# v of five tile pairs by seven half-width products, with staging buffers in the order k, v, q

## The chip, the cores and the metric

The kernel runs on one core of a Trainium2 chip. The metric is the device time in microseconds of one execution; smaller is better.

## The reference

The part that matters is how q, k and v are made and used. `x` has 2048 rows of 512; the weight `wqkv` has 512 columns each for q, k and v; there are 32 heads of 16, and each row attends to 8 rows of its past, two apart.

```python
xn = layernorm(x)                                  # 2048 x 512
q, k, v = split(xn @ wqkv)                         # 512 x 1536, 32 heads of 16
logits = einsum("bhsd,bhswd->bhsw", q, k[s - 2*w]) * 16**-0.5     # w = 0..7, masked at the start
o = einsum("bhsw,bhswd->bhsd", softmax(logits), v[s - 2*w])
s = o @ wo                                         # 512 x 512
h = relu(xn @ w1 + b1) ** 2                        # 1792 wide
out = x + s * silu(h @ w2 + b2)
```

## The kernel before

**Tiles and stages.** The rows are 16 tiles of 128. The first stage normalizes tiles, transposes them, and multiplies them by `wqkv`; from tile 2 on it takes them in pairs (2, 4, ... 14). q, k and v go to DRAM through staging buffers `stg` (a ring of four; 128 partitions, both tiles of a pair) and come back in another layout as the attention's units of 256 rows. The second stage is the feed-forward part in four chunks of 512 rows, with the attention on VectorE (DVE) beside it and the output products `pw` at the end of each chunk.

**Precision.** Every operand of a matmul is split in a high part, rounded by ScalarE (ACT), and a low part, the rest, subtracted by DVE or GpSimd (POOL). A product of high and low parts takes three matmuls, `PASSES`: high by high, high by low, low by high. So the low part of x is wanted from the third matmul on, the low part of a weight from the second.

**The pair of seven.** Pairs 4 to 14 (`SEVEN`, L43) compute q and k together as a product of 2 by 2 blocks: rows of tile a and of tile b, halves of the contraction (`part_x(t, 0)` and `part_x(t, 1)`), columns of q and of k. By Winograd's scheme this takes seven block products instead of eight, each of six matmuls of 512 columns (`product`, L536). The scheme needs sums of x blocks (`sums`, L504, on DVE from PSUM; their parts by `high_sums` on ACT and `low_sums` on DVE) and four sums of weights, T1 to T4, made by DVE and POOL before pair 2 and split during it (`split_sum`, low halves on POOL). The text counts the products of a pair in the order of the code:

1. x of a, first half, by Q0, into `sums_ps`; ACT copies it to `first`, which must be done before product 3 adds to `sums_ps`.
2. the sum S0 by T1, into `five`.
3. S1 by T2, on top of `sums_ps`; evacuated as u, into a buffer of its own (`u2`).
4. x of a, second half, by Q1, on top of `first`: q of tile a.
5. S2 by T3, on top of `sums_ps`; POOL adds it to k of tile b.
6. S3 by K1, on top of `five`; DVE adds u: k of tile a. k is stored.
7. x of b by T4, on top of `sums_ps`: q of tile b. q is stored.

v of the two tiles is computed beside that by `qkv(t, 2)` (L551): 12 matmuls of 512 columns a tile, into a bank of its own, evacuated by ACT.

**What sets the order.** Every engine runs its instructions in the order in which the code issues them (`Ordered`, L75; `queue` does it for SyncE's transfers), and each waits for its operands. Between products stands `beside(a, step)` (L735), which first issues what a table has for that place (`at`, L700), then `pump(LATE)` (L371): as much of the attention as a planner's two clocks, one for TensorE and one for DVE, leave room for. The table makes the statistics, the norms, the transposes (`trans`, `highx`, `lowx`) and the sums for later pairs. At place (2, 2) it has `trans(4)`, `trans(5)`, `stats(6)`, `stats(7)`, `norm(6)` and the split of T3; at (2, 3) `highx`, `norm(7)` and the split of T4; at (2, 4) `lowx(4)`, the sums of x for pair 4 and `spread(8)`; at (2, 5) their rest and `spread(9)`. `spread(t)` (L418) is the statistics of a tile on ACT: a Copy and a Square with an accumulator each, whose 512-wide results are not used, and three small operations on POOL.

**The banks.** PSUM has eight banks: four for accumulators (`psA`), two for `psH`, two for transposes. The raw weights of v, `raws[2]`, lie in the buffer that the attention's v tiles take later. Buffers 10 and `K0` are taken by the pieces 0 and 1 of the feed-forward weights (`next_w`, L394; `HOME`, L41).

Of the kernel before, what the change touches and what calls it, by code (L numbers as in the profile page):

```python
# [14 lines left out]
P = 128  # L15
S = 2048
D = 512
# [25 lines left out]
SEVEN = range(4, 16, 2)  # L43

# [7 lines left out]
MATMUL, TRANSPOSE, DVE_FIXED, SHARED, SLACK, LATE, ROOM0, ROOM = 227, 150, 150, 200, 500, 3000, 500, 3500  # L52
# [5 lines left out]
def body(ctx: ExitStack, tc: tile.TileContext, x, wqkv, wo, w1, b1, w2, b2, out):  # L58
# [5 lines left out]
    def price(engine, name, a, k):  # L64
        if engine == "PE":
            return MATMUL if name == "matmul" else TRANSPOSE
# [178 lines left out]
    def attention():  # L245
# [121 lines left out]

    stream = attention()
# [167 lines left out]
    def product(ps, lhs, w, start=True):  # L536

        k = 0
        for i in range(2):
            for p, q in PASSES:  # L540
                PE.matmul(ps, lhs(p, i), wq[w][:, q, i, :], start=start and k == 0, stop=k == 5,
# [3 lines left out]
    def heads(ps):  # L545
        return ps.rearrange("p (g c) -> p g c", g=GR)
# [4 lines left out]
    def qkv(t, s, between=None, late=False):  # L551
# [10 lines left out]
        evacuate(t, s, ps)  # L562

    def evacuate(t, s, ps):
        if t % 2 == 0:
# [122 lines left out]

    qkv(1, 2)
# [38 lines left out]
    for i, w in enumerate((T2, T3, T4)):  # L728
        at(2, 1 + i, split_sum, w, G)
    for i in range(2):  # L730
        at(4, i, load_w, i)

    ahead = {(10, 2): 1, (12, 4): 1, (14, 0): 1, (14, 2): 1, (14, 4): 1}

    def beside(a, step):  # L735
# [3 lines left out]
        for n in range(ahead.get((a, step), 0)):  # L739
            next_w()  # L740
        pump(LATE)
# [15 lines left out]
    def pair_of_seven(a):  # L757

        b, last = a + 1, a + 2 == NT
        new_stg(a, 1)  # L760
        new_stg(a, 0)
        q, k = stgs[0], stgs[1]
        sums_ps, first, five = (psA(f"pm{a}_{n}") for n in range(3))
        home = dict(pool=px, tag="x", bufs=4) if last else dict(pool=hpool, tag="hf")
        u2 = home.pop("pool").tile([P, GR, CH], F32, name=f"u2_{a}", **home)
# [10 lines left out]
        A.activation(q[:, :, 0], heads(first), AF.Copy)  # L776
        beside(a, 2)
# [234 lines left out]
```

## Time and profile before

| | us |
|---|---|
| median of 3 runs (487.14 to 488.4) | 487.44 |
| profiled execution | 488.73 |
| its span (first to last instruction) | 486.8 |
| TensorE busy | 478.8 (98%) |
| VectorE busy | 417.6 (86%) |
| ScalarE busy | 235.1 (48%) |
| GpSimd busy | 204.1 (42%) |
| pairs 4 to 12 | 41.8 to 119.6 |

Times in the views are microseconds from the span's start. PE is TensorE's matmuls, PEld its weight loads, DVE VectorE, ACT ScalarE, POOL GpSimd, SP SyncE. A group's row gives output and input by the program's names, partitions by elements, the count, busy time and the mean in ns, then the engine's idle time just before it and what ended it. A row of a timeline gives start and length; several like instructions in a row are merged (x4). Matmuls are pipelined: one takes some 0.39 us from start to end, but the next starts earlier, so the pace is read from long rows. All instructions of the main engines carry the line of a helper (L87), so they are told apart by names: `pm` is a pair's products, `pq` a plain `qkv`, `pb` and `ph` the feed-forward part, `pr` and `pv` the attention's products on DVE, `S` and `Sf` the sums of x, `wqraw` raw weights and their sums, `wq` weight parts, `xt` x parts.

### The profile page before, as it was taken

What the parts mean: (1) busy time and instruction counts of PE and PEld (TensorE: products, weight loads), DVE (VectorE), ACT (ScalarE), POOL (GpSimd) and SP (SyncE); (2) the same over time, 40 slices, a digit from 0 to 9 for tenths busy, and PEclk for the clock granted to TensorE, in tenths of its full rate; (3) what the DMA queues carried; (4) which work ended last, traced back from release to release, by engine and by line L of the source; (5) the groups of instructions that cost most, each with busy time, mean ns of one, the idle gap of its engine ahead of it and who ended that gap; (6) DMA issues with size and microseconds to landing.
All of it is one profiled execution on the core that took longest, in us unless ns stands there. A gap on an engine that the chain in (4) does not pass through costs nothing.

```text
span 486.8 us, 5931 instructions
## 1 busy us (share of the span) xinstructions
PE 478.8 (98%) x2118; PEld 393.8 (81%) x2118; DVE 417.6 (86%) x348; ACT 235.1 (48%) x421; POOL 204.1 (42%) x166
## 2 busy tenths in 40 slices
PE   8999999999999999999999999999999999999996
PEld 5888788886888888888888888888888888888885
DVE  5967968986869699999999999999989999959533
ACT  5548697645575576453422444343233543423240
POOL 1347232132756699235534332653524145353210
PEclk9999999999999999999999999999999999999999
DMA  7999999898757992943708184425723852330142
GB/s 278 248 247 275 308 303 260 200 277 276 218 160 197 254 226 91 254 130 68 193 18 200 53 227 139 102 86 125 182 72 71 270 125 86 82 102 27 49 138 76
DMA packets 71002, 81.47 MB, mean 167 GB/s; under 512 B 6204, under 2 KB 55612, under 8 KB 70972
## 3 DMA queue, kind: packets, MB, share of 16 engines
q1 hardware_dynamic: 65788, 54.87, 40.8%
q10 hardware_dynamic: 5184, 26.22, 22.1%
q8 instruction: 17, 0.28, 0.3%
q14 instruction: 13, 0.11, 0.1%
HBM read 50.60 MB, written 27.32 MB: 160 GB/s over the span
## 4 chain that ended last, share of the span: by engine, by line
PE 87%; DMA 5%; DVE 4%; ACT 2%; issue 1%; SPq 0%; POOL 0%; DVEq 0%; ACTq 0%; POOLq 0%
PE pb L87 31%; PE ph L87 31%; PE pq L87 10%; PE pw L87 9%; PE pm L87 5%; DMA sk<-stg 2%; DMA sx<-xt 1%; DVE L L87 1%; DMA xb<-xn 1%; DMA x<-in_A_x 1%; DVE pxT L87 1%; SPq L100 0%; ACT stg L87 0%; DVE pr L87 0%; ACT mean L87 0%
## 5 line engine op out<-in xcount | busy, mean ns | idle before, releaser
L87 PE MATMUL pb<-w,h 128*128 128x512 f32 x672 | 160.1, 389 | 0.0
L87 PEld LDWEIGHTS pb<-w,h 128*128 128x128 f32 x672 | 126.1, 188 | 26.2
L87 POOL TENSOR_TENSOR h<-hf,h 128x512 fp32r<-128x512 f32 x46 | 72.5, 1576 | 152.0 <-ACT hf L87 152.0
L87 PE MATMUL ph<-xU,w 128*128 128x512 f32 x504 | 120.2, 389 | 0.0
L87 ACT ACTIVATE ph<-ph,b1t 128x512 f32<-128x512 f32 x56 | 37.0, 661 | 161.4 <-PE ph L87 152.7
L87 PEld LDWEIGHTS ph<-xU,w 128*128 128x128 f32 x504 | 94.6, 188 | 19.6
L87 DVE TENSOR_TENSOR pr<-k,q 128x2048 f32<-128x2048 f32 x32 | 78.9, 2466 | 4.4 <-DMA q<-sq 3.9
L87 DVE TENSOR_TENSOR pv<-v,L 128x2048 f32<-128x2048 f32 x32 | 75.4, 2355 | 6.3 <-POOL L L87 5.5
L87 DVE TENSOR_REDUCE v<-pv 128x256 f32<-128x2048 f32 x32 | 73.0, 2281 | 0.8
L87 DVE TENSOR_REDUCE L<-pr 128x128 f32<-128x2048 f32 x32 | 72.9, 2279 | 0.7
L87 PE MATMUL pw<-wot,oT 128*128 128x512 f32 (+1 forms) x204 | 45.9, 376 | 0.0
L87 PEld LDWEIGHTS pw<-wot,oT 128*128 128x128 f32 x204 | 36.8, 188 | 7.1
L87 PE MATMUL ph<-xT,w 128*128 128x512 f32 x168 | 40.0, 389 | 0.0
L87 PE MATMUL pq<-wq,xt 128*128 128x512 f32 x144 | 36.0, 392 | 1.7 <-ACT stg L87 1.7
L87 PEld LDWEIGHTS ph<-xT,w 128*128 128x128 f32 x168 | 31.5, 188 | 6.5
L87 PE MATMUL pm<-wq,S 128*128 128x512 f32 x144 | 35.9, 391 | 0.1
L87 POOL TENSOR_TENSOR w<-w1r,w 128x512 fp32r<-128x512 f32 x14 | 22.4, 1598 | 29.1 <-ACT w L87 29.1
L87 ACT ACTIVATE h<-ph 128x512 fp32r<-128x512 f32 x56 | 33.7, 602 | 1.7
L87 PEld LDWEIGHTS pq<-wq,xt 128*128 128x128 f32 x144 | 26.8, 188 | 8.3 <-ACT stg L87 2.8
L87 PEld LDWEIGHTS pm<-wq,S 128*128 128x128 f32 x144 | 26.8, 188 | 6.4 <-ACT u L87 0.7
L87 PE MATMUL pq<-wq,xT 128*128 128x512 f32 x132 | 30.9, 393 | 0.0
L87 PEld LDWEIGHTS pq<-wq,xT 128*128 128x128 f32 x132 | 24.5, 188 | 5.8 <-ACT xT L87 0.7
(82 smaller groups left out, 486.8 us busy)
## 6 DMA issues: line engine op xcount, KB each, us to landing
k<-sk ACTq DMA_DIRECT2D x8, 960.0 KB, 7.4
v<-sv ACTq DMA_DIRECT2D x8, 960.0 KB, 7.5
sx<-xt SPq DMA_DIRECT2D x12, 512.0 KB, 5.7
xU<-sx ACTq DMA_DIRECT2D x12, 512.0 KB, 7.2
x<-in_A_x SPq DMA_DIRECT2D x16, 256.0 KB, 6.3
sk<-stg SPq DMA_DIRECT2D x8, 512.0 KB, 4.3
sq<-stg SPq DMA_DIRECT2D x8, 512.0 KB, 7.3
sv<-stg SPq DMA_DIRECT2D x8, 512.0 KB, 5.0
```

Of the source, the lines that this page charges most:

```text
L87: return tc.keep_in_program_order(f(*a, **k))
```

## The change

v of tiles 4 to 13 (pairs 4 to 12, `VSEVEN`) is computed as q and k are, with blocks of 256 columns: the left and right half of v take the places of q and k. So a pair has seven more products of six matmuls, each 256 wide (`cols`), in place of 24 matmuls of 512. The v product n stands right behind product n (`first_v` is the first, with its copy to `v_first`; `sixth` is product 5 with its evacuation and POOL's add, `seventh` product 6 with DVE's add and the store of k). The four sums of v's weights are made on DVE at place (2, 2), in place in `raws[2]` (`sum_v`), and split at (2, 4), (2, 5), (4, 0) and (4, 1) (`split_v`: high parts ACT, low parts POOL) into buffers 10 and K0. The splits of the feed-forward pieces 0 and 1 move from (10, 2) and (12, 4) to (12, 3) and (12, 5), and the first load of an attention v tile waits until place (4, 1) is issued. All three staging buffers of a pair are taken at its start, in the order k, v, q. u goes to k's own buffer. The unused results of `spread` go to a buffer in SBUF, which frees the two `psH` banks for v.

```diff
-MATMUL, TRANSPOSE, DVE_FIXED, ...
+MATMUL, VMATMUL, TRANSPOSE, DVE_FIXED, ... = 227, 120, 150, 150, ...
...
-        yield from load(0, "kqv")
+        yield from load(0, "kq")
...
+                    if u == 0 and s == 1:
+                        while not v_ready:
+                            yield None
+                        yield from load(0, "v")
...
-        A.activation(psH(f"mean{t}"), xins[t], AF.Copy, scale=-1.0 / D, accum_out=means[t])
-        A.activation(psH(f"var{t}"), xins[t], AF.Square, bias=means[t], accum_out=rs[t])
+        waste = hpool.tile([P, 512], F32, name=f"waste{t}", tag="hf")
+        A.activation(waste, xins[t], AF.Copy, scale=-1.0 / D, accum_out=means[t])
+        A.activation(waste, xins[t], AF.Square, bias=means[t], accum_out=rs[t])
...
+    def sum_v(n):
+        dst, a, b = (((0, vl), (0, vr), (0, vl)), ((2, vr), (2, vr), (0, vl)), ((0, vr), (2, vr), (0, vr)),
+                     ((2, vl), (2, vl), (2, vr)))[n]
+        dst, a, b = (raws[2][:, kt:kt + 2, cols] for kt, cols in (dst, a, b))
+        V.tensor_sub(dst, a, b)
+        v_sums[n] = dst
+
+    def split_v(n):
+        i = n // 2
+        if i not in v_parts:
+            v_parts[i] = buffer(f"vsum{i}", (10, K0)[i])
+        split(*(v_parts[i][:, q, :, (vl, vr)[n % 2]] for q in range(2)), v_sums[n], G)
...
+    for a, step, f, n in ((2, 2, sum_v, 0), (2, 2, sum_v, 2), (2, 2, sum_v, 1), (2, 2, sum_v, 3),
+                          (2, 4, split_v, 0), (2, 5, split_v, 1), (4, 0, split_v, 2), (4, 1, split_v, 3)):
+        at(a, step, f, n)
...
-    ahead = {(10, 2): 1, (12, 4): 1, (14, 0): 1, (14, 2): 1, (14, 4): 1}
+    ahead = {(12, 3): 1, (12, 5): 1, (14, 0): 1, (14, 2): 1, (14, 4): 1}
...
+        for s in (1, 2, 0):
+            new_stg(a, s)
+        q, k, v = (stgs[s] for s in range(3))
...
         product(sums_ps, part_x(a, 0), Q0)
         A.activation(first, sums_ps, AF.Copy)
+        if seven:
+            first_v()
         product(five, part_s(a, 0), T1)
         A.activation(k[:, :, 1], heads(five), AF.Copy)
+        if seven:
+            product(v_five[:, vl], part_s(a, 0), v_parts[0], cols=vl)
+            A.activation(v[:, 4:, 1], heads(v_five[:, vl]), AF.Copy)
         beside(a, 0)
-        qkv(a, 2)
-        beside(a, 1)
+        if not seven:
+            qkv(a, 2, new=False)
+            beside(a, 1)
         product(sums_ps, part_s(a, 1), T2, False)
-        A.activation(u2, heads(sums_ps), AF.Copy)
+        A.activation(k[:, :, 0], heads(sums_ps), AF.Copy)
+        if seven:
+            product(v_sums_ps[:, vl], part_s(a, 1), v_parts[0], False, vr)
+            A.activation(v[:, 4:, 0], heads(v_sums_ps[:, vl]), AF.Copy)
+            beside(a, 1)
...
+        if seven:
+            sixth()
+            product(v_sums_ps[:, vl], part_s(a, 2), v_parts[1], False, vl)
+            A.activation(v[:, :4, 1], heads(v_sums_ps[:, vl]), AF.Copy)
+            G.tensor_add(v[:, 4:, 1], v[:, 4:, 1], v[:, :4, 1])
+            beside(a, 3)
+            seventh()
+            product(v_five[:, vl], part_s(a, 3), V1, False, vr)
+            not_before(clock["PE"])
+            V.tensor_add(v[:, 4:, 0], v[:, 4:, 0], heads(v_five[:, vl]))
...
+        if seven:
+            product(v_sums_ps[:, vl], part_x(b, 1), v_parts[1], False, vr)
+            A.activation(v[:, :4, 1], heads(v_sums_ps[:, vl]), AF.Copy)
+            store_qkv(b, 2)
         store_qkv(b, 0)
```

More of the change, by code (lines that the diff above doesn't have):

```diff
@@ L43 @@
 SEVEN = range(4, 16, 2)
+VSEVEN = range(4, 14, 2)
 WARM = 18
@@ L50 @@
 STATS = 8
[L52 removed]
+MATMUL, VMATMUL, TRANSPOSE, DVE_FIXED, SHARED, SLACK, LATE, ROOM0, ROOM = 227, 120, 150, 150, 200, 500, 3000, 500, 3500
 BEHIND, FREE, LAND, LOAD = 5000, 2000, 4500, 10500
@@ L534, in part_s, with product @@
         return lambda p, i: Sp[a, j // 2][:, p, j % 2, i]
-    def product(ps, lhs, w, start=True):
+    def product(ps, lhs, w, start=True, cols=slice(0, 512)):
         k = 0
+        w = wq[w] if isinstance(w, int) else w
         for i in range(2):
             for p, q in PASSES:
-                PE.matmul(ps, lhs(p, i), wq[w][:, q, i, :], start=start and k == 0, stop=k == 5,
+                PE.matmul(ps, lhs(p, i), w[:, q, i, cols], start=start and k == 0, stop=k == 5,
                           skip_group_check=True)
@@ L545, in heads, with qkv @@
     def heads(ps):
-        return ps.rearrange("p (g c) -> p g c", g=GR)
+        return ps.rearrange("p (g c) -> p g c", c=CH)
     def new_stg(t, s):
         stgs[s] = pstg.tile([P, GR, 2, CH], F32, name=f"stg{t}_{s}", tag="stg", bufs=4)
-    def qkv(t, s, between=None, late=False):
+    def qkv(t, s, between=None, late=False, new=True):
         ps = psA(f"pq{t}_{s}")
@@ L561, in qkv, with evacuate @@
                 between()
-        evacuate(t, s, ps)
-    def evacuate(t, s, ps):
-        if t % 2 == 0:
+        evacuate(t, s, ps, new)
+    def evacuate(t, s, ps, new=True):
+        if t % 2 == 0 and new:
             new_stg(t, s)
@@ L740, in beside @@
             next_w()
+        if (a, step) == (4, 1):
+            v_ready.append(True)
         pump(LATE)
```

43 lines of the change are left out of this document (29 added, 14 removed).

## The prediction

> **What bounds the kernel now.** I read the page first, then the table of stretches for the five pairs that the change rewrites (one row each, start and end of the pair's matmuls), then the timelines of single engines around places where TensorE waits.
>
> ```profile
> PE 478.8 (98%) x2118; PEld 393.8 (81%) x2118; DVE 417.6 (86%) x348; ACT 235.1 (48%) x421; POOL 204.1 (42%) x166
> ...
> PE 87%; DMA 5%; DVE 4%; ACT 2%; issue 1%; SPq 0%; POOL 0%; DVEq 0%; ACTq 0%; POOLq 0%
> ...
> L87 PE MATMUL pq<-wq,xt 128*128 128x512 f32 x144 | 36.0, 392 | 1.7 <-ACT stg L87 1.7
> ```
> ```profile
> 41.78:56.88 15.10, 15.10 (x67) 12.26 (x66) 12.99 (x16) 10.58 (x23) 8.09 (x9) 1.00 1.10 309
> 56.88:72.80 15.92, 15.32 (x67) 12.31 (x66) 11.16 (x19) 15.07 (x35) 5.09 (x13) 1.00 1.10 295
> 72.80:87.87 15.07, 15.07 (x67) 12.31 (x66) 12.68 (x15) 11.08 (x25) 4.81 (x8) 1.00 0.81 219
> 87.87:102.83 14.96, 14.96 (x67) 12.39 (x66) 12.74 (x20) 9.47 (x18) 4.67 (x3) 1.00 1.10 266
> 102.83:119.56 16.73, 15.58 (x67) 12.23 (x66) 12.54 (x15) 6.89 (x14) 1.29 (x1) 1.00 0.94 270
> ```
>
> TensorE is busy 98% of the span and carries 87% of the chain, so a microsecond taken from its work, or added to its waits, is a microsecond of the result. Columns of the table: stretch, length, busy time and count for PE, PEld, DVE, ACT, POOL, then granted clock, DMA share, GB/s. A pair without a wait takes 14.96 us (pair 10). Pairs 6 and 12 take 15.92 and 16.73: 0.96 and 1.77 us of waiting.
>
> **Streaming.** The price of a full matmul comes from the chain in order of time, that of a half-width one from the last two output products, which are 256 wide already.
>
> ```profile
> 458.36 2.72 PE pb L87 x12
> ```
> ```profile
> L87 PE MATMUL pw<-wot,oT 128*128 128x256 f32 x24 | 3.0, 283 | 0.0
> ```
> ```profile
> 480.10:482.50 2.40, 2.40 (x23) 2.40 (x22) 2.18 (x4) 0.00 (x0) 0.00 (x0) 1.00 0.05 11
> ```
>
> A 512-wide matmul costs 2.72/12 = 0.227 us. Of 24 half-width ones, 23 steps fit into 3.0 - 0.28 us: 0.118; some 20 whole steps in 2.40 us say 0.120, and the weight loads (x22, busy without a gap) set that pace, not the columns. I take 0.120. A pair's v goes from 24 x 0.227 = 5.44 us to 7 x 6 x 0.120 = 5.04: 0.40 less, over five pairs **-2.0 us**. By the Trainium skill (TensorE: Matmul & The Clock Gate, Back-to-back issue gap) a warm matmul of N columns is spaced N/2.4 + 2.5 ns, 109 ns here; by that estimate the five pairs would save 4.3 us, but the rows above show 120, bound by the loads.
>
> **Waits that may go.** Before 112 us the v evacuation held ACT, and TensorE behind it:
>
> ```profile
> 111.57 0.60 ACT L87 ACTIVATE stg<-pq 128x512 f32<-128x512 f32 x1 [5.22 <-DMA sk<-stg]
> ```
>
> v's staging buffer was still being stored. In the new pair v's first write comes after the fourth group of matmuls (1.36 + 0.72 + 1.36 + 0.72 = 4.2 us), and v's sums have banks of their own, so ACT can be several us late without stopping TensorE. Of the 2.73 us in pairs 6 and 12 I take **-2.3** (between 0 and -2.7).
>
> **The entry to pair 4.** Here the change adds work to three queues that are already late. DVE must still make, in this order, norm(6), the four subtractions for v's weight sums, norm(7), lowx(4), and the sums of x that pair 4 multiplies.
>
> ```profile
> 36.94 0.69 DVE L87 BATCH_NORM_STATS2 st<-x 128x6 f32<-128x512 f32 x1 [2.13 <-DMA x<-in_A_x]
> ...
> 37.95 0.54 DVE L87 TENSOR_SCALAR xn<-x,mv,rs 128x512 f32<-128x512 f32 x1
> 38.94 1.51 DVE L87 TENSOR_SCALAR xn<-x,mv,rs 128x512 f32<-128x512 f32 x1 [0.44 <-POOL rs L87]
> 40.38 0.68 DVE L87 TENSOR_TENSOR xt<-pxT,xt 128x512 fp32r<-128x512 f32 x1
> ...
> 45.61 2.29 DVE L87 TENSOR_TENSOR pr<-k,q 128x2048 f32<-128x2048 f32 x1
> ```
> ```profile
> 38.88 5.69 POOL L87 TENSOR_TENSOR wq<-wqraw,wq 128x512 fp32r<-128x512 f32 x4
> 44.65 0.19 POOL L87 TENSOR_SCALAR rs<-rs 128x1 f32<-128x1 f32 x1
> 44.92 0.55 POOL L87 TENSOR_TENSOR rs<-rs,mhalf 128x1 f32<-128x1 f32 x1
> 45.55 0.19 POOL L87 TENSOR_TENSOR shift<-mean,rs 128x1 f32<-128x1 f32 x1
> 46.52 1.43 POOL L87 TENSOR_SCALAR rs<-rs 128x1 f32<-128x1 f32 x1 [0.77 <-ACT var L87]
> ```
> ```profile
> L87 DVE TENSOR_TENSOR wqraw<-wqraw,wqraw 128x512 f32<-128x512 f32 x6 | 3.7, 683 | 0.0
> ```
>
> norm(6) frees DVE at about 38.4. A subtraction of 512 elements costs 3.7/6 = 0.6 us when alone, so four would be 2.5 us. They are not alone: at 38.88 POOL begins the four low halves of T3 and T4 (5.69 us). What such a meeting does is shown at 121 us, DVE's and POOL's timelines:
>
> ```profile
> 121.24 0.68 DVE L87 TENSOR_TENSOR L<-L,sm 128x256 f32<-128x256 f32 x1
> 121.84 3.38 DVE L87 TENSOR_TENSOR pr<-k,q 128x2048 f32<-128x2048 f32 x1
> ```
> ```profile
> 121.60 1.47 POOL L87 TENSOR_TENSOR w<-w2r,w 128x512 fp32r<-128x512 f32 x1
> 123.68 2.70 POOL L87 TENSOR_TENSOR w<-w1r,w 128x512 fp32r<-128x512 f32 x1 [0.60 <-ACT w L87]
> ```
>
> pr takes 2.29 us at 45.61 and 3.38 here, ending 2.15 us after POOL's subtraction ended at 123.07; POOL's next one, issued at 123.68, ends at 126.38, 1.2 us after pr. And POOL got in between two DVE operations that stood back to back. So operations that read two SBUF operands go one at a time and in turn. The Trainium skill (SBUF — State Buffer, Who interferes with whom) says the same, that the shared pair is held for a whole instruction and the other engine blocks fully; the rows agree, and it is a rule that speaks against this placing.
>
> In turn, then: first subtraction to 39.0, POOL to 40.25, DVE to 40.8, POOL to 42.05, DVE to 42.6, POOL to 43.85, DVE to 44.4, POOL to 45.65 (1.25 and 0.55 each), and norm(7), which waited for POOL in the same way (1.51), to 45.95. lowx(4) starts at 45.9 instead of 40.38: **5.5 us later**. The ends: 1.0 if DVE keeps its turn four times and norm(7) then meets no POOL operation (38.4 + 2.5 + 0.5 = 41.4), 6 if POOL always goes first. The rows at 121 us are the nearest; I take 5.5.
>
> What waits for it:
>
> ```profile
> 41.78 1.52 PE L87 MATMUL pm<-wq,xt 128*128 128x512 f32 x6
> ...
> 47.36 1.52 PE L87 MATMUL pm<-wq,S 128*128 128x512 f32 x6
> ```
> ```profile
> 41.87 0.63 ACT L87 ACTIVATE S<-Sf 128x512 fp32r<-128x512 f32 x1 [1.95 <-DVE Sf L87]
> ...
> 43.78 0.19 ACT L87 ACTIVATION_READ_ACCUMULATOR var<-x,mean 128x1 f32 x1
> 43.87 0.58 ACT L87 ACTIVATE stg<-pq 128x512 f32<-128x512 f32 x1
> 44.35 0.62 ACT L87 ACTIVATE S<-Sf 128x512 fp32r<-128x512 f32 x1
> ...
> 46.24 0.19 ACT L87 ACTIVATION_READ_ACCUMULATOR var<-x,mean 128x1 f32 x1
> 46.34 0.58 ACT L87 ACTIVATE pm<-pm 128x512 f32<-128x512 f32 x1
> ```
>
> Pair 4's first product needs the low part of x from its third matmul on (41.78 + 0.45 = 42.23); it comes at 46.6, and TensorE stands 4.3 us. ACT's queue hangs on DVE's sums (idle 1.95 until 41.87), so its whole row above moves by 5.5, and two new high parts of v's sums (0.52 each, as 43.87 to 44.35 and 44.35 to 44.87 go) stand ahead of the copy of the first product: 46.34 + 5.5 + 1.04 = 52.9, done at 53.5. In the old order that copy was wanted at 47.36, now before product 3, and product 3 now stands earlier: without waits at 45.94. POOL: the second group of small operations starts when var(9) is there (46.43 + 5.5 + 0.52 = 52.45), takes 1.1 us (44.65 to 45.74), then the low part of split_v(1) 1.3: 54.9. The third v product needs it, and ends at 55.6. Without waits it ends at 41.78 + 3 x 1.36 + 3 x 0.72 = 48.0. The entry costs **+7.6 us**. With no delay on DVE at all, ACT's two new operations alone make the copy ready at 46.9 + 1.04 = 47.95, where 45.94 is wanted: +2.0. That is the lower end. The upper: a pr in front of POOL's group (46.52 took 1.43 instead of 0.19, because pr ran) adds 1.4: 9.0.
>
> **At nothing.** A pair's evacuations on ACT become six of 256 instead of two of 512, on DVE one add is new, on POOL one. Each result is wanted 2.8 us or more after its product, and ACT has 4 us free in pairs 8 and 10; were the cover gone, each late 0.4 us evacuation would show as such.
>
> ```profile
> L87 ACT ACTIVATE Sf<-pxT 128x256 f32<-128x256 f32 x6 | 2.4, 403 | 0.0
> ```
>
> The statistics' waste goes from PSUM to SBUF at equal length. DVE's extra 4.5 us (4 x 0.6, 5 x 0.42) meets a tail with room: the last low part ends at 470.6, its tile's products start one product after 477.24, which leaves over 6 us. The v load of unit 0 goes behind pair 4's second step; cover is the rest of unit 0's logits on DVE, and its price if needed at once is its landing, 7.5 us. The splits of weight pieces 0 and 1, moved to pair 12, go past no evacuation that product 7 waits for, and the loads of pieces 2 and 3 that they start are wanted after pair 14. u in k's own buffer is the same ACT copy to another place.
>
> ```profile
> 469.91 0.69 DVE L87 TENSOR_TENSOR oT<-pT,oT 128x512 fp32r<-128x512 f32 x1 [1.32 <-ACT oT L87]
> ```
> ```profile
> 477.24 5.75 PE L87 MATMUL pw<-wot,oT 128*128 128x512 f32 x36
> ```
> ```profile
> v<-sv ACTq DMA_DIRECT2D x8, 960.0 KB, 7.5
> ```
>
> **Sum.** -2.0 - 2.3 + 7.6 = +3.3 us. Against the profiled execution (488.73: span 486.8 and 1.9 around it) that is 492.0; that execution lies 1.3 above the median of 487.44, so in terms of the median **490.7**.
>
> **Rivals.** *The turns do not alternate* (0.38). DVE's four subtractions run through while POOL waits: the delay is 0 to 1.0 and the entry costs 2.0 to 3.0 us, or POOL gets in once or twice, 3.0 to 5.5. For it: four DVE operations of one kind, each ready when the last ends. Against: pr at 121.84 was ready too and waited. With 2.0 and the waits gone the time is 487.4 - 4.3 + 2.0 = 485.1, faster; with 4.3 it is no change. The point is an entry of 2.8 us, 485.9: below it the change wins by over 0.3% (about what a measurement of this kernel can tell from no change). I give the faster part 0.21, the middle 0.17. *The entry drops TensorE's clock* (0.10). The last row of stretches shows the clock at 0.51 after 2.4 us without matmuls:
>
> ```profile
> 485.40:486.80 1.40, 0.00 (x0) 0.00 (x0) 0.00 (x0) 0.00 (x0) 0.00 (x0) 0.51 0.00 0
> ```
>
> A stop of 4.3 us is longer. If the clock takes as long to come back as the stop lasted, 4.3 us at half pace lose 2.1, unless they fall into the waits that follow: 492.8. The Trainium skill (TensorE: Matmul & The Clock Gate, The HAM clock gate) gives one idle window of about 3.4 us for the fall and as much work for the rise; by that estimate it would be 1.7 us, and the 0.51 agrees with its idle state. *The DMA waits move* (0.07). v now takes the buffer from which the last pair's k is stored; if that lands 1 us too late in each of four pairs and the old 2.3 stays: 490.7 + 2.3 + 4 = 497.
>
> **How the numbers follow.** Main case 0.45, its own range 489.0 to 492.6; with the two slow rivals slower gets 0.62. Faster 0.21, same 0.17. The range, 485.0 to 493.0, reaches from the lower end of the first rival to the clock's case; the DMA case and what lies outside both ends are left out.
>
> **What would show it.** 256-wide pm and pv matmuls at 0.120; the four wqraw subtractions on DVE spread over 5 to 6 us between POOL's; lowx(4) near 46; TensorE idle in the first product of pair 4 and before its second and third v product; pairs 6 to 12 at 14.6 us. Wrong would be: subtractions 0.6 us apart, or a pair 4 under 17 us.

## The result, and the profile after

The changed kernel is slower by 1.28%: 494.4 us (median of 4 runs, 494.05 to 494.89) against 487.9 on the same chip, a ratio of 1.0128 with the interval 1.0097 to 1.0159. Its profiled execution took 494.3 us, span 492.5; the one before had 488.73 and 486.8. From the first matmul of pair 14 to the last of the kernel both take 363.2 us, and pair 4 starts at 41.8 in both, so the whole difference between the two profiled executions lies in the five pairs that were rewritten.

The table of stretches of the changed kernel, pairs 4, 6, 8, 10 and 12 (stretch, length, busy time and count of PE, PEld, DVE, ACT, POOL, then granted clock, DMA share, GB/s):

```profile
41.80:66.24 24.44, 17.11 (x86) 14.07 (x85) 17.44 (x24) 16.51 (x37) 15.91 (x17) 0.93 0.72 186
66.24:80.94 14.70, 14.70 (x87) 12.90 (x86) 12.77 (x16) 13.13 (x32) 4.73 (x11) 1.00 0.93 255
80.94:95.79 14.85, 14.85 (x86) 12.96 (x85) 14.55 (x20) 12.26 (x29) 5.92 (x10) 1.00 1.05 256
95.79:110.49 14.70, 14.70 (x87) 12.90 (x85) 14.10 (x21) 9.32 (x20) 5.15 (x4) 1.00 1.04 279
110.49:125.19 14.70, 14.70 (x87) 12.90 (x85) 11.76 (x14) 8.53 (x20) 3.78 (x4) 1.00 0.99 286
```

Before they took 15.10, 15.92, 15.07, 14.96 and 16.73, 77.78 in all; now 83.39, or 5.61 more, which is the difference of the two profiled executions (5.57). Four pairs became shorter by 3.7 together, and pair 4 longer by 9.3. The page shows the same as a small loss of TensorE's share and a dent in the fourth and fifth slice:

```profile
PE 479.4 (97%) x2208; PEld 398.6 (81%) x2208; DVE 427.3 (87%) x357; ACT 242.4 (49%) x445; POOL 221.4 (45%) x175
PE   8996799999999999999999999999999999999996
PEclk9998999999999999999999999999999999999999
```

Pair 4 on TensorE's timeline (start, length, operation, what ended the idle time before it):

```profile
41.80 0.61 PE L90 MATMUL pm<-wq,xt 128*128 128x512 f32 x2
46.75 2.08 PE L90 MATMUL pm<-wq,xt 128*128 128x512 f32 x4 [4.33 <-DVE xt L90]
48.62 1.40 PE L90 MATMUL pv<-wq,xt 128*128 128x256 f32 x6
50.65 1.65 PE L90 MATMUL pm<-wq,S 128*128 128x512 f32 x6 [0.63 <-ACT stg L90]
52.14 0.87 PE L90 MATMUL pv<-vsum,S 128*128 128x256 f32 x6
53.64 1.66 PE L90 MATMUL pm<-wq,S 128*128 128x512 f32 x6 [0.62 <-ACT pm L90]
55.13 0.28 PE L90 MATMUL pv<-vsum,S 128*128 128x256 f32 x1
57.15 0.86 PE L90 MATMUL pv<-vsum,S 128*128 128x256 f32 x5 [1.75 <-POOL vsum L90]
57.85 1.54 PE L90 MATMUL pm<-wq,xt 128*128 128x512 f32 x6
```

There are four stops: the first is ended by DVE, the next two by ACT, the last by POOL. After that nothing holds the pair. An undisturbed full product and the half-width one behind it take 2.10 together (14.70/7), so the fourth product would start at 41.80 + 3 x 2.10 = 48.10; it starts at 57.85. The entry costs 9.75 us.

### The profile page after: what moved, and what is told of

Read it like the earlier page. It is cut to its first block, busy times and chain, and to the rows that moved or that the text cites. A ratio compares the mean times of both kernels' runs of the same rounds, so it can differ in the third digit from the quotient of the medians.

```text
span 492.5 us, 6172 instructions
## 1 busy us (share of the span) xinstructions
PE 479.4 (97%) x2208; PEld 398.6 (81%) x2208; DVE 427.3 (87%) x357; ACT 242.4 (49%) x445; POOL 221.4 (45%) x175
## 4 chain that ended last, share of the span: by engine, by line
PE 90%; DMA 4%; DVE 2%; ACT 1%; POOL 1%; issue 0%; SPq 0%; POOLq 0%; ACTq 0%
PE pb L90 31%; PE ph L90 31%; PE pm L90 11%; PE pw L90 9%; PE pv L90 5%; PE pq L90 4%; DMA x<-in_A_x 2%; DMA sq<-stg 2%; DVE wqraw L90 1%; POOL vsum L90 1%; DVE xn L90 0%; ACT waste L90 0%; DVE st L90 0%; PE pxT L90 0%; POOL rs L90 0%
## 5 line engine op out<-in xcount | busy, mean ns | idle before, releaser
L90 POOL TENSOR_TENSOR h<-hf,h 128x512 fp32r<-128x512 f32 x46 | 83.8, 1822 | 138.7 <-ACT hf L90 137.9
L90 PE MATMUL pw<-wot,oT 128*128 128x512 f32 (+1 forms) x204 | 45.9, 376 | 0.0
L90 PE MATMUL pm<-wq,S 128*128 128x512 f32 x144 | 37.1, 394 | 1.2 <-ACT stg L90 0.6
L90 POOL TENSOR_TENSOR w<-w1r,w 128x512 fp32r<-128x512 f32 x14 | 26.0, 1860 | 18.9 <-ACT w L90 16.3
L90 PE MATMUL pm<-wq,xt 128*128 128x512 f32 x108 | 29.1, 404 | 4.3 <-DVE xt L90 4.3
L90 PEld LDWEIGHTS pm<-wq,S 128*128 128x128 f32 x144 | 25.8, 189 | 6.1 <-ACT stg L90 0.8
L90 ACT ACTIVATE hf<-ph 128x512 f32<-128x512 f32 x46 | 27.3, 594 | 1.9 <-POOL h L90 1.9
```

Of the source, the lines that this page charges most:

```text
L90: return tc.keep_in_program_order(f(*a, **k))
```

## Where pair 4 lost its time

DVE's timeline, and POOL's beside it:

```profile
38.94 5.75 DVE L90 TENSOR_TENSOR wqraw<-wqraw 128x512 f32<-128x512 f32 x4
44.61 1.48 DVE L90 TENSOR_SCALAR xn<-x,mv,rs 128x512 f32<-128x512 f32 x1
46.01 0.68 DVE L90 TENSOR_TENSOR xt<-pxT,xt 128x512 fp32r<-128x512 f32 x1
...
53.72 2.26 DVE L90 TENSOR_TENSOR pr<-k,q 128x2048 f32<-128x2048 f32 x1
```
```profile
39.41 6.40 POOL L90 TENSOR_TENSOR wq<-wqraw,wq 128x512 fp32r<-128x512 f32 x4
...
52.67 0.19 POOL L90 TENSOR_SCALAR rs<-rs 128x1 f32<-128x1 f32 x1 [0.64 <-ACT waste L90]
...
53.72 4.63 POOL L90 TENSOR_TENSOR vsum<-wqraw,vsum 128x512 fp32r<-128x512 f32 x2
```

The four subtractions take 5.75 us beside POOL's four low halves, and `lowx(4)` starts at 46.01: the turns, as forecast (45.9). The last row of POOL is new. There the low part of `split_v(1)` starts in the same moment as DVE's `pr` and stands behind it; it ends at about 57.1. The row has two such operations in 4.63 us; in other kernels two take 2.5 us when nothing holds them. TensorE's last stop ends then, at 57.15. ACT's timeline joins the two ends:

```profile
47.51 0.63 ACT L90 ACTIVATE S<-Sf 128x512 fp32r<-128x512 f32 x1 [7.57 <-DVE Sf L90]
...
49.50 0.61 ACT L90 ACTIVATE vsum<-wqraw 128x512 fp32r<-128x512 f32 x1
50.02 0.58 ACT L90 ACTIVATE stg<-pq 128x512 f32<-128x512 f32 x1
...
52.49 0.62 ACT L90 ACTIVATE vsum<-wqraw 128x512 fp32r<-128x512 f32 x1
53.01 0.58 ACT L90 ACTIVATE pm<-pm 128x512 f32<-128x512 f32 x1
```

ACT is idle 7.57 us for the sums of x (1.95 before). Then come a spread, a new high part and only then `stg<-pq`, the evacuation of pair 2's last product; the second product of pair 4 (50.65) takes the bank that this one empties. Another spread and another new high part stand ahead of `pm<-pm`, the copy of the first product, which releases the third (53.64). Where the forecast had one late copy on ACT, there are two. From 47.51 to 53.5 ACT works without a gap, and POOL's small operations wait for ACT and not for TensorE; so the low part comes at 57.1 however early TensorE gets there, and the last stop, not the sum of the four, sets the 9.75.

The clock fell as well. A stretch of the same table, just behind the first stop:

```profile
46.70:49.70 3.00, 2.95 (x10) 2.57 (x10) 2.69 (x6) 2.16 (x6) 0.02 (x1) 0.50 0.72 146
```

Ten matmuls (the rest of the first product and its half-width one) ran at half the granted clock. At full pace they would have ended at about 48.4 (4 x 0.227 + 0.72 from 46.75) instead of 50.0; since the next product waited until 50.65 anyway, nothing of this reached the end.

## The experiments

The pair lengths of all kernels, from their profiled executions, with the sum of the five, the median time, and the ratio to the kernel before on the same chip (the experiments ran on several chips, where the kernel before took 487.85 to 488.15):

| kernel | pair 4 | 6 | 8 | 10 | 12 | sum | median | ratio (interval) |
|---|---|---|---|---|---|---|---|---|
| before | 15.10 | 15.92 | 15.07 | 14.96 | 16.73 | 77.8 | 487.9 | 1 |
| changed | 24.44 | 14.70 | 14.85 | 14.70 | 14.70 | 83.4 | 494.4 | 1.0128 (1.0097 to 1.0159) |
| order alone | 15.31 | 15.67 | 15.78 | 14.96 | 14.96 | 76.7 | 487.98 | 1.0006 (0.9987 to 1.0025) |
| no low halves of T3, T4 | 17.42 | 14.70 | 14.85 | 14.70 | 14.70 | 76.4 | 487.86 | 0.9997 (0.9983 to 1.0012) |
| sums earlier | 20.16 | 14.70 | 14.84 | 14.69 | 14.82 | 79.2 | 490.2 | 1.0057 (1.0031 to 1.0084) |
| no sums | 19.09 | 14.70 | 17.45 | 15.97 | 14.70 | 81.9 | 494.31 | 1.0129 (1.004 to 1.0217) |
| no sums, priced | 20.41 | 14.70 | 14.85 | 14.70 | 14.70 | 79.4 | 491.25 | 1.0072 (1.0046 to 1.0098) |
| `split_v(1)` first | 22.75 | 14.70 | 14.85 | 14.69 | 14.70 | 81.7 | 493.52 | 1.0109 (1.0072 to 1.0145) |
| early sums and splits | 19.25 | 14.70 | 14.85 | 14.70 | 14.70 | 78.2 | 489.47 | 1.0038 (1.002 to 1.0057) |
| from pair 6 | 14.99 | 16.50 | 14.70 | 14.70 | 14.70 | 75.6 | 487.03 | 0.9981 (0.9965 to 0.9998) |
| from 6, end of 4 later | 15.33 | 16.49 | 14.70 | 14.70 | 14.70 | 75.9 | 486.79 | 0.9977 (0.9958 to 0.9996) |
| from 6, one spread less | 14.99 | 14.98 | 15.64 | 14.70 | 14.70 | 75.0 | 486.75 | 0.9969 (0.995 to 0.9987) |
| from 6, two by two | 15.09 | 16.50 | 15.40 | 14.64 | 14.81 | 76.4 | 487.31 | 0.9983 (0.9959 to 1.0006) |

**Order alone: everything but the products.** Staging order, u, waste, the later load of v and the later splits stay; the half-width products, their sums and splits go.

```diff
-VSEVEN = range(4, 14, 2)
+VSEVEN = range(0)
...
-    for a, step, f, n in ((2, 2, sum_v, 0), (2, 2, sum_v, 2), (2, 2, sum_v, 1), (2, 2, sum_v, 3),
-                          (2, 4, split_v, 0), (2, 5, split_v, 1), (4, 0, split_v, 2), (4, 1, split_v, 3)):
-        at(a, step, f, n)
```

> The changed kernel without its half-width products: v by two plain products of 12 full matmuls a tile as before, no sums of v's weights; the staging order k, v, q, u in k's buffer, the waste in SBUF, the later v load and the later feed-forward splits stay. Theory (the waits of pairs 6 and 12 went because v is written later and has its own banks): they are still there, pairs 4 to 12 take together 77 to 78.5 us, the time is 487 to 489. Rival (the staging order alone frees the buffer in time): pairs 6 and 12 come down to 15.0, the time is 485 to 486.

It took 487.98 us, no change to measure, as the theory had it. The pairs divide it from the rival less clearly: their sum is 76.7, below the 77 to 78.5 of the theory, because the wait of pair 12 is not in this profile (14.96), while those of ACT in pair 6 and now pair 8 are (15.67 and 15.78). So the rearrangement without the products neither costs nor brings anything that can be measured in the time.

**No low halves of T3 and T4.** POOL does not make them; products 5 and 7 take the high half in their place.

```diff
+        only_high = isinstance(w, int) and w in (T3, T4)
...
-                PE.matmul(ps, lhs(p, i), w[:, q, i, cols], start=start and k == 0, stop=k == 5,
+                PE.matmul(ps, lhs(p, i), w[:, 0 if only_high else q, i, cols], start=start and k == 0, stop=k == 5,
...
-            split(*sum_weights[w, i], eng)
+            (high(*sum_weights[w, i]) if w in (T3, T4) else split(*sum_weights[w, i], eng))
```

> The changed kernel without POOL's four low halves of T3 and T4; products 5 and 7 use the high half in the low half's place, so q and k are less exact. DVE's four subtractions stay where they are. Theory (turns): the subtractions stand 0.6 us apart, 2.5 us in all, norm(7) is not held either, lowx(4) starts near 42; POOL has no queue, so the low parts of v's sums come earlier too; the time is 487 to 489. Rival (the subtractions are slow by themselves, for instance because they write over what they read): still 5 to 6 us in all, lowx(4) near 46, the time above 492.

The subtractions on DVE's timeline, without POOL beside them:

```profile
37.94 2.87 DVE L90 TENSOR_TENSOR wqraw<-wqraw 128x512 f32<-128x512 f32 x4
41.18 0.68 DVE L90 TENSOR_TENSOR xt<-pxT,xt 128x512 fp32r<-128x512 f32 x1
```

They take 2.87 us instead of 5.75, `norm(7)` behind them is not held either, and `lowx(4)` starts at 41.18 instead of 46.01. Pair 4 falls from 24.44 to 17.42, and the time to that of before. These 7.0 us are not the turns alone, for the run also takes 5.7 to 6.4 us of work out of POOL's queue. POOL's low part of `split_v(1)` comes just ahead of `pr`, and this time it is `pr` that waits (DVE, then POOL):

```profile
48.97 3.36 DVE L90 TENSOR_TENSOR pr<-k,q 128x2048 f32<-128x2048 f32 x1
```
```profile
48.88 1.30 POOL L90 TENSOR_TENSOR vsum<-wqraw,vsum 128x512 fp32r<-128x512 f32 x1
```

So the run shows that the subtractions are slow only beside POOL; the next runs, which keep POOL's work, give the price. The 2.7 that remain here are the two waits for ACT (1.60 and 0.61) and some 0.5 in restarting behind them.

**Sums earlier.** The four subtractions stand between `stats(6)` and `stats(7)`, ahead of POOL's low halves.

```diff
+            if (t, i) == (6, 0):
+                for n in (0, 2, 1, 3):
+                    at(a, step, sum_v, n)
-    for a, step, f, n in ((2, 2, sum_v, 0), (2, 2, sum_v, 2), (2, 2, sum_v, 1), (2, 2, sum_v, 3),
-                          (2, 4, split_v, 0), (2, 5, split_v, 1), (4, 0, split_v, 2), (4, 1, split_v, 3)):
+    for a, step, f, n in ((2, 4, split_v, 0), (2, 5, split_v, 1), (4, 0, split_v, 2), (4, 1, split_v, 3)):
```

> The changed kernel with the same four subtractions issued between stats(6) and stats(7), where DVE stands 2.4 us for x of tile 7 and POOL waits for stats(7). All work is kept. Theory (turns with POOL): the four take 2.4 to 2.6 us in all instead of 5.75, lowx(4) starts between 40.9 and 41.5, the time is within 0.7 us of the run without them, 488 to 490. Rival (the price is the amount of DVE work ahead of lowx(4), whatever its place): lowx(4) starts near 43.5, the time is near 492.

DVE, TensorE and POOL of this kernel, and a stretch of its table:

```profile
35.18 2.86 DVE L90 TENSOR_TENSOR wqraw<-wqraw 128x512 f32<-128x512 f32 x4
41.39 0.68 DVE L90 TENSOR_TENSOR xt<-pxT,xt 128x512 fp32r<-128x512 f32 x1
...
48.50 2.27 DVE L90 TENSOR_TENSOR pr<-k,q 128x2048 f32<-128x2048 f32 x1
```
```profile
46.02 1.90 PE L90 MATMUL pm<-wq,S 128*128 128x512 f32 x6 [1.86 <-ACT stg L90]
...
52.99 0.86 PE L90 MATMUL pv<-vsum,S 128*128 128x256 f32 x5 [1.13 <-POOL vsum L90]
```
```profile
48.58 2.23 POOL L90 TENSOR_SCALAR rs<-rs 128x1 f32<-128x1 f32 x1
```
```profile
47.30:50.70 3.40, 2.99 (x11) 2.29 (x10) 3.40 (x3) 3.11 (x8) 3.31 (x2) 0.50 1.11 367
```

The turns are gone and pair 4 takes 20.16, 4.3 less, with all work kept; that prices the turns. The pair is still 5.5 above an undisturbed one, where the changed kernel has 9.7, and the time, 490.2, is just above the 488 to 490 that were expected. TensorE is held by ACT's evacuation of pair 2's last product (1.86) and by POOL behind `pr` (an operation on one element a partition, 0.19 alone, takes 2.23 and pushes back the low part behind it). The second of these decides: the third v product cannot go on before 52.99, when that low part is there. The clock was at half for 3.4 us here too, but ahead of that stop, which it only shortened.

**No sums.** The four subtractions are left out.

```diff
-        V.tensor_sub(dst, a, b)
```

> The changed kernel without the four DVE subtractions that make v's weight sums; the raw halves are split and multiplied in their place, so v of tiles 4 to 13 is not the reference's. Nothing else differs. Theory (the subtractions and POOL's low halves of T3 and T4 take turns at a shared port, and all of pair 4's entry hangs on that): lowx(4) starts near 40.9 us instead of 46.0, the wait in pair 4's first product (4.3 us) is gone, and what stays at the entry is ACT's two new operations and POOL's first two low parts, 3 to 5 us instead of 9.9; the time falls from 494.4 by 5 to 6.5 us, to 488 to 489.5. Rival (the entry is set by ACT's and POOL's own new work, the DVE delay is only the first to be met): the third v product still waits until about 57, the time stays above 493.

Pair 4 fell to 19.09, but the time (two executions) stayed. Pairs 8 and 10 grew by 4.0 together, and ACT's timeline shows a wait for the store of v, in pair 10, that no other kernel has at this length:

```profile
105.48 0.60 ACT L90 ACTIVATE stg<-pm 128x512 f32<-128x512 f32 x1 [4.17 <-DMA sv<-stg]
```

The planner prices each operation of DVE; without the four it placed the attention's work earlier, and the first load of v left at 71.2 instead of 85.3. That this load is what made the store late is argued from the next run, which has neither. A DMA wait was the third rival of the prediction; here the experiment brought it in. The run does not tell what the subtractions cost, and so was repeated with the price kept.

**No sums, priced.** The same, with the planner's clock for DVE still charged.

```diff
-        V.tensor_sub(dst, a, b)
+        clock["V"] += 512 / 0.96 + DVE_FIXED
```

> Left out: the four VectorE subtractions that make the v weights' sums (v of tiles 4 to 13 is therefore not the reference's); the planner still charges VectorE's clock with their price, so that the places of the loads and stores stay those of the changed kernel. Theory (the turns with GpSimd make pair 4 late, and the long pairs 8 and 10 of the kernel without the sums came from its earlier load of v): x(4)'s low part is ready at about 40.2 us, pair 4 takes about 19.0, pairs 6 to 12 take 14.7 to 14.85 each, and the time is about 489.0 (5.3 below the changed kernel). Rival (the missing subtractions themselves move work into pairs 8 and 10): these stay at 17.4 and 16.0 and the time stays near 493 to 494.

The long pairs 8 and 10 are gone, as the theory had it, and the time is 491.25 us, 2.2 above what it had. Pair 4 takes 20.41 instead of 19.0: after the third v product's stop (2.13 us, for POOL behind `pr` again) eleven matmuls run at half pace. TensorE's timeline and one stretch:

```profile
51.67 1.06 PE L90 MATMUL pv<-vsum,S 128*128 128x256 f32 x5 [2.13 <-POOL vsum L90]
52.53 2.76 PE L90 MATMUL pm<-wq,xt 128*128 128x512 f32 x6
```
```profile
52.50:55.00 2.50, 2.50 (x8) 2.01 (x7) 0.00 (x0) 1.61 (x3) 0.91 (x2) 0.50 0.08 29
```

A product of six takes 2.56 (52.53 to 55.09) instead of 1.39. So POOL behind `pr` costs something even with DVE free, and the clock falls behind that stop.

**`split_v(1)` first.** The changed kernel, with the second half of the first v split issued ahead of `spread(9)`.

```diff
+            if (t, i) == (8, 1):
+                at(a, step, split_v, 1)
...
-                          (2, 4, split_v, 0), (2, 5, split_v, 1), (4, 0, split_v, 2), (4, 1, split_v, 3)):
+                          (2, 4, split_v, 0), (4, 0, split_v, 2), (4, 1, split_v, 3)):
```

> Same work as the changed kernel; the second half of the v split is issued ahead of the spread of pair 8's last statistics in VectorE's and GpSimd's order, so that GpSimd's low part no longer stands behind that spread. Theory (the last link of pair 4's delay is this low part, 53.72 us and 4.63 long for two because it turns with the spread): it ends before 53.5 us, the third v product is not held at 55.1, pair 4 takes about 22.4 instead of 24.4, and the time is about 492.3. Rival (the delay is set by the stop in the first product and the clock after it alone): pair 4 stays at 24.4 and the time at 494.3.

The mechanism held: the low part was done by 53.42 (start 50.45, 2.97 for two), and the wait of the third v product went. From the start of the third product to that of the fourth it is now 2.10 us (54.27 to 56.37) instead of 4.21 (53.64 to 57.85), so this link is worth 2.1. The sizes did not all follow: pair 4 took 22.75 where 22.4 was expected, and the time was 493.52 and not 492.3. In the pair the gain is 1.7: the first stop was 0.5 shorter in this execution, and the half pace, which lasted to 54.10 here, fell on the second product and took some 0.9 back. The medians lie 0.9 apart, too little to tell from two executions.

TensorE's timeline:

```profile
50.38 2.93 PE L90 MATMUL pm<-wq,S 128*128 128x512 f32 x6 [1.20 <-ACT stg L90]
53.10 1.33 PE L90 MATMUL pv<-vsum,S 128*128 128x256 f32 x6
```

**Early sums and splits.** An attempt to keep pair 4 in the new form with a better order: sums as in "sums earlier", the first two v splits earlier, at (2, 3), the last two one step later, T4 split ahead of T3, whose split moves into pair 4, the spreads of tiles 8 and 9 one step later.

```diff
-    slots = {6: ((2, 2), (2, 2), (2, 2), (2, 3)), 8: ((2, 4), (2, 5), (4, 0), (4, 1)),
+    slots = {6: ((2, 2), (2, 2), (2, 2), (2, 3)), 8: ((2, 5), (4, 0), (4, 0), (4, 1)),
...
-    for i, w in enumerate((T2, T3, T4)):
-        at(2, 1 + i, split_sum, w, G)
+    for a, step, w in ((2, 1, T2), (2, 2, T4), (4, 0, T3)):
+        at(a, step, split_sum, w, G)
...
```

> The changed kernel with the same products in pairs 4 to 12; the four subtractions stand between the statistics of tiles 6 and 7 (before GpSimd's halves of the sums' weights), the first two v splits one step earlier, the weight split T4 ahead of T3, and pair 8's first spreads one step later. Theory (the entry is a queue order and not an amount of work): pair 4 takes 16 to 17 instead of 24.4, pairs 6 to 12 14.7 to 14.85 each, time 485 to 486.5. Rival (the second product of pair 4 waits for ScalarE's evacuation of the pair before anyway, by 1.9 us, and the splits by as much again): pair 4 stays at 19 to 20 and the time at 489 to 490.

The expectation failed: 19.25 and not 16 to 17. The first three products and their half-width ones lose 0.3 us (the fourth starts at 48.46, 6.58 after the first, for 6.30), but then T3's low halves come too late, behind the small operations of a spread that stood behind `pr`. TensorE's timeline, then POOL's:

```profile
52.75 0.96 PE L90 MATMUL pm<-wq,S 128*128 128x512 f32 x3 [1.24 <-POOL wq L90]
53.99 1.21 PE L90 MATMUL pm<-wq,S 128*128 128x512 f32 x2 [0.28 <-POOL wq L90]
```
```profile
48.82 1.76 POOL L90 TENSOR_SCALAR rs<-rs 128x1 f32<-128x1 f32 x1 [1.90 <-ACT waste L90]
...
51.43 2.50 POOL L90 TENSOR_TENSOR wq<-wqraw,wq 128x512 fp32r<-128x512 f32 x2
```

And the clock was at half from 54.04 to 57.45, behind the last stop, where nothing hid it: by the spacing of the matmuls it cost some 1.8 us, the largest part of what is left. Without it the pair would be near 17.5 (an estimate from these rows), still above the expected 16 to 17. So this order does not mend the entry; whether another does was not tried.

**From pair 6.** Pair 4 computes v as before; sums and splits move into it, and the release of the v load to (4, 4).

```diff
-VSEVEN = range(4, 14, 2)
+VSEVEN = range(6, 14, 2)
...
+    for a, step, f, n in ((4, 0, sum_v, 0), (4, 0, sum_v, 2), (4, 0, sum_v, 1), (4, 0, sum_v, 3),
+                          (4, 1, split_v, 0), (4, 2, split_v, 1), (4, 2, split_v, 2), (4, 4, split_v, 3)):
...
```

> The seven half-width products from pair 6 on (tiles 6 to 13); pair 4 computes v as the kernel before does, and the four subtractions and the split of the sums stand in pair 4 after the statistics of tile 6. Theory (the cost is pair 4's entry alone; an undisturbed new pair takes 14.70 and an old one 14.96): pair 4 takes 15.0 to 15.3, four pairs 14.7 to 14.85 each, sum 74.0 to 74.5 against 77.8 before, time 484.0 to 484.7: faster than both kernels. Rival (the subtractions and GpSimd's halves delay whatever pair they stand ahead of): pair 6 opens 3 to 6 late, as pair 4 did, and the time is 487 to 490.

It is faster than the changed kernel and just below the kernel before (0.9981, interval to 0.9998), by less than expected: 487.03 and not 484.0 to 484.7. Pair 4 is back at 14.99, but pair 6 takes 16.50, in one wait. TensorE, and ACT ahead of it:

```profile
62.66 1.65 PE L90 MATMUL pm<-wq,S 128*128 128x512 f32 x6 [1.57 <-ACT stg L90]
```
```profile
60.05 0.62 ACT L90 ACTIVATE waste<-x 128x512 f32<-128x512 f32 x1
...
61.52 0.61 ACT L90 ACTIVATE vsum<-wqraw 128x512 fp32r<-128x512 f32 x1
62.03 0.58 ACT L90 ACTIVATE stg<-pm 128x512 f32<-128x512 f32 x1
```

The old pair's last product is evacuated behind a spread and a split. In this profiled execution the clock reached its full pace only at 10.80 us (4.1 to 7.0 in the other kernels), and the six matmuls that start at 6.96 took 4.74 us where they take 2.84 in the next kernel. So pair 4 starts at 43.87, some 2 us late, and the time is 489.13 where the median is 487.03.

**From pair 6, the end of pair 4 later**, and **one spread less.** Two steps to remove that wait. In the first the spread of tile 10, the last split and the release of the v load are issued behind pair 4's last product; in the second the spread of tile 11 also goes two steps into pair 6.

```diff
-             10: ((4, 4), (4, 5), (6, 0), (6, 1)), 12: ((6, 2), (6, 3), (6, 4), (6, 5)),
+             10: ((4, 5), (4, 5), (6, 0), (6, 1)), 12: ((6, 2), (6, 3), (6, 4), (6, 5)),
...
-                          (4, 1, split_v, 0), (4, 2, split_v, 1), (4, 2, split_v, 2), (4, 4, split_v, 3)):
+                          (4, 1, split_v, 0), (4, 2, split_v, 1), (4, 2, split_v, 2), (4, 5, split_v, 3)):
```
```diff
-             10: ((4, 5), (4, 5), (6, 0), (6, 1)), 12: ((6, 2), (6, 3), (6, 4), (6, 5)),
+             10: ((4, 5), (6, 1), (6, 1), (6, 2)), 12: ((6, 3), (6, 4), (6, 4), (6, 5)),
```

> The kernel with the half-width products from pair 6 on, and in pair 4 the spread of tile 10's statistics, the last split of the v sums' weights and the release of the v load issued after the pair's last product instead of before it. Theory (pair 6's second product stood 1.57 us for ScalarE's evacuation of pair 4's last product, at 62.03 behind a spread and a split that were issued ahead of it, 1.53 and 0.51 us): the evacuation comes at about 60, the wait goes, pair 6 takes 14.7 to 14.9 instead of 16.5, the five pairs sum to 73.8 to 74.2 and the time is 484.3 to 485.5, ratio 0.993 to 0.995. Rival (ScalarE is late from its wait for S, and whatever it does next stands in the way): pair 6 stays above 15.5 and the time at 487.

Here the rival won. The evacuation came at 58.48 (the pairs start 1.9 us earlier here, so that is the theory's 60), and the second product no longer waited; but the third now stood as long for the copy of the first, at the end of the same queue (TensorE):

```profile
63.18 1.65 PE L90 MATMUL pm<-wq,S 128*128 128x512 f32 x6 [1.56 <-ACT pm L90]
```

> The kernel with the half-width products from pair 6 on and the work of pair 4's end moved behind its last product, and with tile 11's statistics spread two steps into pair 6 instead of ahead of its first copy (the steps of tiles 12 and 13 move on by one). Theory (the wait of 1.56 us in pair 6 went from the second product to the third, because ScalarE's copy of the first product stood behind two spreads of 1.6 us each and a split; with one spread less the copy is at about 60.5 instead of 62.56): no wait of over 0.3 us in pair 6, pairs 14.7 to 14.9, sum 74.0 to 74.3, time 485.0 to 485.7, ratio 0.994 to 0.996. Rival (ScalarE has no room in pair 6, the spread only moves the wait to a later product): pair 6 stays at 16 to 16.5 and the time at 486.8.

With the second spread moved too, pair 6 takes 14.98, 0.1 above the expected pair; 0.65 of wait came up in pair 8. It has the lowest time of the study: 486.75 us, ratio 0.9969 (0.995 to 0.9987), so 0.3% below the kernel before, where 485.0 to 485.7 were expected. From the kernel of the step before (486.79, ratio 0.9977 on another chip) its time can't be told apart; only the pairs tell them apart, 75.0 against 75.9. The sum was expected at 74.0 to 74.3, so both theories have a part: most of the wait could be moved into a free place, some came back.

**Two by two.** On the kernel with the end of pair 4 later, the half-width products are taken two by two: 4 groups a pair instead of 7.

```diff
         product(sums_ps, part_x(a, 0), Q0)
         A.activation(first, sums_ps, AF.Copy)
-        if seven:
-            first_v()
         product(five, part_s(a, 0), T1)
         A.activation(k[:, :, 1], heads(five), AF.Copy)
         if seven:
+            first_v()
             product(v_five[:, vl], part_s(a, 0), v_parts[0], cols=vl)
...
```

> Same products as the kernel with the moved spread (half-width from pair 6 on), with the first six of a pair's half-width products taken two by two after two full products: four groups of half-width matmuls in a pair instead of seven. It asks why an undisturbed new pair takes 14.70 and not the 14.56 that 42 half-width matmuls at 0.120 and the rest at 0.227 give. Theory (the six full matmuls after each half-width group run at 0.231 instead of 0.227, 0.028 us a group): three groups less give 0.08, undisturbed pairs of 14.61 to 14.63. Rival (the half-width matmuls themselves cost more, wherever they stand): the undisturbed pair stays at 14.70.

The undisturbed pair 10 takes 14.64 instead of 14.70, 0.06 less where the theory had 0.08. TensorE's timeline there shows a full product alone and two in a row:

```profile
88.86 1.55 PE L90 MATMUL pm<-wq,xt 128*128 128x512 f32 x6
90.25 1.52 PE L90 MATMUL pm<-wq,S 128*128 128x512 f32 x6
91.61 0.88 PE L90 MATMUL pv<-wq,xt 128*128 128x256 f32 x6
92.33 0.88 PE L90 MATMUL pv<-vsum,S 128*128 128x256 f32 x6
```

A full product behind half-width ones lasts 1.39 to the next (88.86 to 90.25), one behind a full product 1.36, a half-width one 0.72 (91.61 to 92.33). The loss lies in the full product behind a change of width, as the theory says; the grouping saves little and made a wait for ACT in pair 8 (15.40).

## Why the prediction was wrong

The sign and all of the mechanism but its last link were forecast, the size was not: 490.7 with a range to 493.0, against 494.4. On the profiled executions it was 492.0 against 494.3.

**Streaming (-2.0): too large.** The half-width matmul's price was right: 0.72 a product and a little less. What the step left out is that the full products behind them became dearer, 1.39 instead of 1.36. Measured per pair: 14.96 to 14.70, so 0.26 and not 0.40, **-1.3** over five. The estimate by the Trainium skill (TensorE: Matmul & The Clock Gate, Back-to-back issue gap), 109 ns, is not borne out here either: the step between half-width matmuls stays at 120. The page gives that formula for an isolated matmul and says that it under-counts at small widths, where every matmul has its own weight load, as here. That the loads set the 120, as the forecast says, no run here tests.

**Waits that may go (-2.3): about right.** All of 2.98 us went in the five pairs' profile (77.78 less 5 x 14.96), but for 0.15 in pair 8 that is new; **-2.8** net. The mechanism is the one forecast: in pair 12 ACT still waits 2.90 us for the store of k (until 117.67), and TensorE does not stop for it. The run with the order alone shows that the size is not solid: it has waits of 0.71 and 0.82 of the same kind in pairs 6 and 8, and no faster time. How much of pair 12's wait an ordinary execution of the kernel before has isn't known; the profiled one lies 0.8 above the median of the runs beside the changed kernel.

**The entry (+7.6): the failed step.** It measured **+9.75**, beyond the upper end of 9.0. Link by link: `lowx(4)` at 46.01 (forecast 45.9), the stop in the first product 4.33 us (4.3), the copy of the first product ready at 53.6 (53.5). The chain was right up to there. The last link was not: POOL's low part of `split_v(1)` was to be done at 54.9, with `pr` in front of it as the upper case, and `pr` came: it is issued at 53.72 beside that very operation, which ends at about 57.1 (3.4 us instead of 1.3). The forecast let ACT's and POOL's rows move by 5.5 us but not DVE's `pr`, which moved with them. The kernel with `split_v(1)` first prices this link at 2.1 us, as much as the entry was missed by (2.15). The wait of the second product for ACT (0.63) wasn't seen at all, because the bank that `five` takes was not followed; it comes ahead of the last stop, here and in the kernel with earlier sums (1.86), so it did not set the size.

**The median (-1.3): did not carry over.** The changed kernel's profiled execution (494.3) lies at its median (494.4), so the correction from profile to median was wrong by its whole size. With 2.2 of the entry it makes the miss of 3.7; the errors of streaming (+0.7) and waits (-0.5) nearly cancel.

**The rivals.** That the turns do not alternate (0.38) is refuted: 5.75 us for four subtractions, 2.87 without POOL. The fall of the clock (0.10) happened and cost nothing in the changed kernel, as its condition said (it fell into the waits that followed); in three of the experiments it cost something (1.2 us on one product in the priced run, some 0.9 with `split_v(1)` first, some 1.8 with early sums and splits). The DMA rival (0.07) did not happen: TensorE has no such wait in pairs 6 to 12. The chance of 0.62 for slower was on the right side; the range was too narrow above, because the upper case of the entry and the clock's case were each priced alone and never with the median left where it was.

## What to carry to other kernels

The gain was 0.26 us a pair and known to be small; the price was paid once, at the place where the new operands are made. Before a stage is made cheaper, place its preparation on the queues that run into it, operation by operation, and move everything that hangs on a late step along with it: here the large DVE operation that was thought to be past came along and stood on POOL. Where the way in is full, start one stage later: with four pairs of five in the new form the time was 0.3% below the kernel before instead of 1.3% above it, though pairs 6 and 8 still took 0.3 and 0.9 us more than an undisturbed one. By the pair lengths, 1.0 of the 2.8 us gained is the streaming; the rest is waits of the kernel before that went.

## What the runs showed of the hardware

- DVE and POOL took turns, operation by operation: DVE's four subtractions, each with two operands in SBUF, took 5.75 us beside POOL's low halves and 2.87 without them; POOL's four took 6.40 beside them and 5.69 in the kernel before. `norm(7)`, with one large operand, was held as well (1.48 instead of 0.54), and a POOL operation of 128 x 1 elements took 2.23 us instead of 0.19 beside `pr`. The Trainium skill (SBUF — State Buffer, Who interferes with whom) says that issue order decides who blocks; the rows agree (POOL waited where `pr` started 0.08 us ahead of it, `pr` where it started 0.09 us behind POOL), and in those rows neither of two ready engines got a second turn in a row.
- A full product behind a half-width one took 1.388 us for its six matmuls, 0.231 each instead of 0.227. Why is open.
- The granted clock changed in steps of one grid: in every trace of this study the times between two changes are whole multiples of 3.413 us (12, 1 and 130 of them in the changed kernel). It fell in pair 4 of five kernels, and the matmuls ran at half pace for one such window (3.41 us), with `split_v(1)` first for two (6.83). A fall comes at the end of a window, so the half pace can begin late: in the kernel with earlier sums 1.2 us after the stop had ended.
- The length of a stop alone doesn't decide whether the clock falls. It fell behind stops of 4.33, 3.84, 2.13 and 1.86 us, and behind three short ones (0.29, 1.24, 0.28), but not behind stops of 2.79 (the kernel without sums), 1.60 and 1.57. Counted within the grid, idleness nearly decides: in the windows that ended with these five falls TensorE was idle for 3.41, 2.62, 2.13, 1.86 and 1.81 us, and no window with 1.64 or less ended with one. The stop of 2.79 us lay in two windows, idle for 1.62 and 1.82 us in all; that the second did not end with a fall is open. The Trainium skill (TensorE: Matmul & The Clock Gate, The HAM clock gate) has a free-running window of about 3.4 us; the grid agrees with that. But the page asks for one idle window before a fall, and 1.81 us of idleness within a window were enough here.
